# Sliding-window attention and gated MLP on one core: another order of the first attention steps, a fifth column group moved once per head, and a last row normed on VectorE

## The chip, the cores and the metric

The kernel runs on one core of a Trainium2 chip. The metric is the device time in microseconds of one execution. A core has five engines with instruction queues of their own: TensorE (PE in the profile, its weight loads PEld), VectorE (DVE), ScalarE (ACT), GpSimd (POOL) and SyncE (SP). SP, POOL and ACT also issue DMAs.

## The reference, cut to what matters

`x` has 2048 rows of 576 values in bf16. Four layers follow each other, A, B, A, B, each added to `x`:

```
def _A_ref(x, wqkv, wo):        # x is layer-normed first
    H = 32; Dh = 18; W, dil = (8, 2)
    q, k, v = split(x @ wqkv)
    idx = pos[:, None] - off[None, :]            # off = 0, 2, ..., 14
    logits = einsum('bhsd,bhswd->bhsw', q, kg) * scale, masked where idx < 0
    attn = softmax(logits);  o = einsum('bhsw,bhswd->bhsd', attn, vg)
    return o @ wo

def _B_ref(x, w_in, w_sp, b_sp, w_out):          # x is layer-normed first
    z = gelu(x @ w_in)                           # 576 -> 4608
    z1 = z[..., :Fh];  z2 = layernorm(z[..., Fh:])
    g = einsum('ts,bsf->btf', w_sp, z2) + b_sp
    return (z1 * g) @ w_out
```

## The kernel before, in words

**Layer A.** The normed input lies transposed in `xnT` (5 chunks of the 576 columns; row blocks of 128). The even and the odd rows of `x` are kept as two halves, so that the dilated window becomes a dense one. Queries and keys of all heads go into the tile `QK` (`[128, 2, 8, 2048]`: keys or queries, eight groups of four heads, rows); the rows of a head that hold no query or key hold a pattern (`win_pat`) which makes the window's mask part of the matrix product.

The way into `QK` has three stages. `PG(d, qk, cc)` computes one column group `d` of 128 columns (`d` = 0 to 4; the fifth has only 64 query and 64 key columns, which are computed together in one product of 128 rows), for keys or queries (`qk`), and one block `cc` of 512 rows, in a PSUM bank `pp`. `evac` copies the bank to a staging tile `stg` (for `d` of 3 and 4 in the first layer it is a piece of `win2a`, lent until that weight is loaded). When a stage is full, a DMA for each head moves its 18 columns to their place in `QK`. Column group 0 holds heads 0 to 7, group 1 heads 7 to 14, group 2 heads 14 to 21, group 3 heads 21 to 28, group 4 heads 28 to 31. For group 4 the keys and queries of a head lie on other partitions of the stage (64 apart), and two DMAs move a head.

The PSUM banks `pp` come from `PT_tile`, a ring: in this part of the layer it is Y, Y, PT, PT, PT, five banks, so that the fifth request after one gets the same bank again. A bank is free again when every instruction that reads it is done.

The attention runs over 17 row tiles and two halves of the heads: step `s` is tile `s // 2` and half `s % 2` (heads 0 to 15, then 16 to 31), 34 steps. `L_mm(s)` multiplies keys by queries into `L_ps`, `EXP(s)` takes the exponential on ACT, `PV(s)` multiplies by the values, and DVE divides by the sums. In the loop, step `s` issues `L_mm(s+1)`, `EXP(s+1)`, `PV(s)` and then what a table holds for the step: the remaining `PG` of rows 1024 to 2047, `VW` (values of a tile), `WO` (output product), loads and stores. `L_mm(0)` and `EXP(0)` stand between the `PG` units of the list `pre`, ahead of the loop.

Everything in the layer is in `manual_schedule`: each engine takes its instructions in the order in which the code issues them.

The first layer (`li == 0`) begins with layer norms: `S_` (statistics, `B_` and `G_`), `R_` (the reciprocal root, its power on POOL), `A_` (norm on DVE), then a transpose on PE (`T_pe`) or by DMA on SP's queue (`T_`). `rows[2]` and `rows[3]` build the mask pattern, `load_pat` loads it, and `fill_window_rows(QK, 0)` writes it into half of `QK` with copies on DVE (L198). What follows on each queue there is set by these lines:

```
            self.fill_window_rows(QK, 0)
            S_(13, 14, 15)
            order = [(d, cc) for cc in range(2) for d in range(5)]
            for k_, (d, cc) in enumerate(order):
                for qk in ((1, 0) if d < 4 else (0,)):
                    PG(d, qk, cc, False, ...)
```

`False` is the argument `dve`: ACT evicts. In the second layer A (`li == 2`) the first sixteen units run in two groups of eight by `PG_run`, whose third argument lists the units that DVE evicts (the others are ACT's); then come

```
            self.fill_window_rows(QK, 1)
            for cc in range(2):
                PG(4, 0, cc, False, q2)
```

and eight `VW` units. In the first layer `fill_window_rows(QK, 1)` stands in the list `pre`, behind its fourth unit.

**Layer B.** `p1` (z2 with its norm), `p2` (z1 and the gate product, most of the time) and `p3`, the out stage: 16 row blocks, for each the product with `w_out`, the residual sum on DVE (`p3_finish`), and, when another layer A follows, the layer norm of the new row: statistics on DVE (`ln_stats`; the power and `nmr`, the negated mean times the reciprocal root, on POOL), the norm on ACT (`ln_xn`), and the transpose into `xnT`. The transpose of the last row block is issued inside the next layer A, between its two groups.

Of the kernel before, what the change touches and what calls it, by code (L numbers as in the profile page):

```python
# [63 lines left out]
class K:  # L64
# [275 lines left out]
    def layer_A(self, li):  # L340
# [44 lines left out]
        def q0_(t):  # L385
            return cfg.tiles[t][0]
# [55 lines left out]
        def PG(d, qk, cc, dve, queues=(nc.sync, nc.gpsimd), pp=None):  # L442
# [14 lines left out]
            if pp is None:  # L457
                pp = self.PT_tile([P, 512], f32, "pp")[:, :]
                for c in range(5):
                    PG_mm(pp, d, qk, cc, c, c == 0, c == 4)  # L460
            evac(stg[:, qk, gi * 512:(gi + 1) * 512], pp, dve)
            stg_left[key] -= 1
            if stg_left[key] == 0:
                stg_tiles.pop(key)
                cs = slice(cc * 512, (cc + 1) * 512) if alone else slice(cb * CBW, (cb + 1) * CBW)
                ss = slice(gi * 512, (gi + 1) * 512) if alone else slice(0, CBW)
                moves = []
                for h in range(d * P // DH, H):
                    a, b = max(h * DH, d * P), min((h + 1) * DH, (d + 1) * P)
                    if a >= b:  # L470
                        break
                    g, rg = divmod(h, 4)
                    q0, s0, n = 32 * rg + a - h * DH, a - d * P, b - a
                    if d < 4:
                        moves.append((QK[q0:q0 + n, :, g, cs], stg[s0:s0 + n, :, :]))
                    else:
                        for a_ in range(2):
                            moves.append((QK[q0:q0 + n, a_, g, cs], stg[64 * a_ + s0:64 * a_ + s0 + n, 0, ss]))
                for dst, src in moves:
                    dma_rr[0] += 1  # L480
                    self.dma(dst, src, eng=queues[dma_rr[0] % len(queues)])

        NST = 2 * NT
        L_tiles = {}
        owed = []
# [15 lines left out]
        def EXP(s):  # L501
            nk, nq = tdim(s // 2)
            for jp, L_ps in enumerate(L_tiles.pop(s)):
                Lv = L_ps[:].rearrange("p a (b c) -> p a b c", c=P)
                nc.scalar.activation(out=P_bufs[2 * jp + s % 2][:nk, :, :, 0:nq], in_=Lv[:nk, :, :, 0:nq], func=ACT.Exp,  # L505
                                     scale=scale)
# [4 lines left out]
        def PV(s):  # L511
# [3 lines left out]
            for jp, js in enumerate(((0, 1, 2), (3,))):  # L515
                for ftl in range(4):
                    for jj, j in enumerate(js):
                        idx = 4 * ftl + j
                        nc.tensor.matmul(O_ps[:, idx * (DH + 1):(idx + 1) * (DH + 1)],  # L519
                                         lhsT=P_bufs[2 * jp + s % 2][:nk, jj, ftl, :],  # L520
                                         rhs=v_ext[:nk, t, 16 * hf + idx, :], start=True, stop=True)
# [112 lines left out]
        if li == 0:  # L634
# [74 lines left out]
            for i in range(3):  # L709
# [5 lines left out]
                for t, hh in (((0, 0),), ((0, 1),), ((1, 0), (1, 1)))[i]:  # L715
                    VW(t, hh, False)
            B_(4)
            A_(3)
            G_(4)
            T_pe(3)  # L720
            for t in (2, 3):
                for hh in range(2):
                    VW(t, hh, False)
            x3 = sb.tile([P, 4, D], bf16, name="x_in3", tag="x_in", bufs=2)
            x_load(x3[:], 12, 4, nc.sync)
            stgs.append(x3[:].rearrange("p a b -> p (a b)")[:, 0:2 * CBW].rearrange("p (a b) -> p a b", a=2))
            S_(5)
            R_(4, 2)
            rows[2](nc.sync)
            A_(4, 5)  # L730
# [24 lines left out]
        else:  # L755
# [3 lines left out]
            for d0 in (0, 2):  # L759
                PG_run([(d, qk, cc) for d in (d0, d0 + 1) for cc in range(2) for qk in (1, 0)], qs,  # L760
                       (0, 1, 5, 7) if d0 == 0 else (1, 3, 5, 7),
                       None if d0 == 0 else lambda: nc.vector.memset(wqk4[64:128, :], 0.0))
# [40 lines left out]
        for k_, (t, hh) in enumerate(vws):  # L803
            assert vsteps[k_] <= 2 * t - 2 + hh
            at(vsteps[k_], VW, t, hh, vsteps[k_] >= PG_END - 2 and k_ % 2 == 0)
# [4 lines left out]
        for t in range(NT - 2):  # L810
            s = wo_steps[q0_(t) // P][0] - 1
            r = (q0_(t) + tdim(t)[1] - 1) // P - RING
            if t < NT - 3 and not in_ring(t):
                at(min(2 * t + 6, s), O_CP, t)
                assert r < 0 or wo_steps[r][1] < min(2 * t + 6, s)
            else:
                assert r < 0 or wo_steps[r][1] < 2 * t + 1
        tail_rows = []
# [37 lines left out]
        for k_, (d, qk, cc) in enumerate(pre):  # L856
            if k_ == (2 if li == 0 else 0):
                self.ring = ["PT"]
                L_mm(0)
                EXP(0)  # L860
# [26 lines left out]
    def layer_B(self, li):  # L887
# [259 lines left out]
        def p3_finish(i, acc):  # L1147
# [108 lines left out]
```

## Time and profile before

| what | value |
|---|---|
| time, median of 3 runs | 1162.35 us (1161.28 to 1163.54) |
| the profiled execution's own time | 1164.2 us |
| its span, first to last instruction | 1162.4 us |
| mean granted TensorE clock | 0.997 |
| PE busy | 1146.0 us (99%), 8163 instructions |
| DVE, ACT, POOL busy | 559.4 us, 339.0 us, 271.0 us |
| first layer A | 0 to about 125 us |
| first layer B | to about 588 us, its out stage from 517 us |
| second layer A | to about 696 us |
| second layer B | to the end |

A row of the timeline has the start, the busy time, the engine, the line of the kernel, the operation, what it writes and reads, how many instructions are merged in the row, and, in brackets, how long the engine was idle ahead of it and what released it. A row of the windows has the busy time of each engine in a stretch with its number of instructions, then the granted clock, the share of the DMA engines and their rate. A row of the chain has the start, the length and the work.

### The profile page before, as it was taken

What the parts mean: (1) busy time and instruction counts of PE and PEld (TensorE: products, weight loads), DVE (VectorE), ACT (ScalarE), POOL (GpSimd) and SP (SyncE); (2) the same over time, 40 slices, a digit from 0 to 9 for tenths busy, and PEclk for the clock granted to TensorE, in tenths of its full rate; (3) what the DMA queues carried; (4) which work ended last, traced back from release to release, by engine and by line L of the source; (5) the groups of instructions that cost most, each with busy time, mean ns of one, the idle gap of its engine ahead of it and who ended that gap; (6) DMA issues with size and microseconds to landing.
All of it is one profiled execution on the core that took longest, in us unless ns stands there. A gap on an engine that the chain in (4) does not pass through costs nothing.

```text
span 1162.4 us, 19969 instructions
## 1 busy us (share of the span) xinstructions
PE 1146.0 (99%) x8163; PEld 610.5 (53%) x8258; DVE 559.4 (48%) x1183; ACT 339.0 (29%) x503; POOL 271.0 (23%) x375
## 2 busy tenths in 40 slices
PE   9899999999999999999999999999999999999998
PEld 5467544444444444457755774444444444444677
DVE  8679888322233222235475888862322223322321
ACT  5499455011110111102247884541011110011000
POOL 3769855000000000001163776540000000000000
PEclk9899999999999999999999999999999999999999
DMA  9599796000000000049656997920000000001332
GB/s 214 114 177 291 199 219 132 23 12 12 12 2 11 12 12 1 19 138 297 172 102 117 229 245 183 259 55 4 8 12 12 12 12 1 12 1 47 114 104 74
DMA packets 184600, 106.59 MB, mean 92 GB/s; under 512 B 136201, under 2 KB 165545, under 8 KB 184509
## 3 DMA queue, kind: packets, MB, share of 16 engines
q1 hardware_dynamic: 171821, 86.04, 32.4%
q0 software_dynamic: 6096, 13.38, 4.4%
q10 hardware_dynamic: 6592, 5.90, 1.7%
q8 instruction: 64, 1.05, 0.4%
q14 instruction: 27, 0.22, 0.1%
HBM read 42.54 MB, written 21.77 MB: 55 GB/s over the span
## 4 chain that ended last, share of the span: by engine, by line
PE 94%; issue 1%; POOL 1%; ACT 1%; DVE 1%; DMA 1%; SPq 0%; ACTq 0%; DVEq 0%; POOLq 0%
PE pg L1094 43%; PE po L1143 12%; PE pz L946 6%; PE pz L1070 6%; PE pz1s L1070 6%; PE pzs L946 6%; PE pp L422 5%; PE pw L587 3%; PE O_ps L519 3%; PE pv L411 3%; PE L_ps L496 2%; POOL QK L78 1%; ACT P_sb L505 1%; DMA x_in<-in_A_x_dram 0%; DVE QK L198 0%
## 5 line engine op out<-in xcount | busy, mean ns | idle before, releaser
L1094 PE MATMUL pg<-Wq,Z 128*128 128x512 bf16 x2260 | 497.9, 379 | 2.5
L1094 PEld LDWEIGHTS <-Z 128*128 128x128 bf16 x2304 | 225.4, 98 | 271.8
L1098 DVE TENSOR_TENSOR g_tmp<-pg,ln_xn 128x512 f32<-128x512 f32 x144 | 99.6, 692 | 420.8 <-PE pg L1094 418.8
L1089 ACT ACTIVATE z1T<-pz 128x1024 bf16<-128x1024 f32 x36 | 34.9, 1021 | 500.8 <-PE pz L1070 500.8
L78 POOL DMA_DIRECT2D wout<-in_B_w_out_dram x4 | 4.3, 1073 | 598.8 <-PE pg L1094 598.8
L1143 PE MATMUL po<-wout,Z 128*128 128x288 bf16 x1152 | 141.4, 286 | 0.0
L505 ACT ACTIVATE P_sb<-L_ps 128x1440 bf16<-128x1440 f32 (+3 forms) x136 | 125.1, 972 | 23.0 <-PE L_ps L496 21.4
L1143 PEld LDWEIGHTS <-Z 128*128 128x128 bf16 x1152 | 112.7, 98 | 28.8
L946 PEld LDWEIGHTS <-xnT 128*128 128x128 bf16 (+1 forms) x800 | 68.2, 97 | 75.3 <-issue 9.7
L1099 DVE TENSOR_TENSOR Z<-g_tmp,z1T 128x512 bf16<-128x512 f32 x144 | 99.7, 692 | 13.0 <-DVE g_tmp L1098 0.9
L995 DVE BATCH_NORM_STATS2 z_st<-zp 128x6 f32<-128x512 bf16 (+1 forms) x160 | 91.5, 618 | 14.6 <-ACT zp L993 14.3
L1070 PEld LDWEIGHTS <-w 128*128 128x128 bf16 (+1 forms) x640 | 53.7, 97 | 74.0 <-issue 13.6
L422 PE MATMUL pp<-xnT,wqk_sb 128*128 128x512 bf16 (+1 forms) x313 | 76.4, 385 | 1.1 <-issue 0.2
L1153 DVE TENSOR_TENSOR x_new<-po,xo 128x288 f32<-128x288 f32 (+1 forms) x64 | 28.8, 455 | 88.4 <-PE po L1143 82.6
L1070 PE MATMUL pz<-xnT,w 128*128 128x512 bf16 (+1 forms) x316 | 66.3, 380 | 0.2
L1070 PE MATMUL pz1s<-xnT,w 128*128 128x512 bf16 (+1 forms) x310 | 64.9, 379 | 0.9 <-issue 0.8
L258 POOL TENSOR_SCALAR ln_xn<-x_new,ln_mv,ln_rstd 128x576 bf16<-128x576 f32 x28 | 64.1, 2289 | 2.6
L946 PE MATMUL pzs<-win2a,xnT 128*128 128x512 bf16 (+1 forms) x235 | 58.6, 358 | 0.4 <-issue 0.3
L946 PE MATMUL pz<-win2a,xnT 128*128 128x512 bf16 (+1 forms) x233 | 58.3, 357 | 0.4
L993 ACT ACTIVATE zp<-pz 128x1024 bf16<-128x1024 f32 (+2 forms) x56 | 36.6, 720 | 64.5 <-PE pz L946 64.5
L1019 POOL TENSOR_SCALAR Z<-zp,z_mv,z_rstd 128x256 bf16<-128x256 bf16 x32 | 54.4, 1701 | 3.8 <-POOL z_rstd L1011 0.4
L78 POOL DMA_DIRECT2D QK<-stg x76 | 46.9, 621 | 35.2 <-DVE stg L403 17.2
(124 smaller groups left out, 951.6 us busy)
## 6 DMA issues: line engine op xcount, KB each, us to landing
xres<-x_new SPq DMA_DIRECT2D x44, 288.0 KB
xo<-xres SPq DMA_DIRECT2D x32, 288.0 KB
wout<-in_B_w_out_dram POOLq DMA_DIRECT2D x4, 1296.0 KB, 7.9
xn_rows<-ln_xn SPq DMA_DIRECT2D x28, 160.0 KB
w<-in_B_w_in_dram SPq DMA_DIRECT2D x16, 256.0 KB
QK<-stg POOLq DMA_DIRECT2D x51, 72.0 KB, 4.7
xo<-xres SPq DMA_DIRECT2D x6, 576.0 KB
QK<-stg SPq DMA_DIRECT2D x37, 72.0 KB
```

Of the source, the lines that this page charges most:

```text
L78: return eng.dma_start(out=out, in_=in_)
L258: e.tensor_scalar(out=xn[:nrows, 0:D], in0=x_t[:nrows, :], scalar1=mv[:nrows, 0:1], scalar2=rstd[:nrows, 0:1], op0=ALU.subtract, op1=ALU.mult)
L422: nc.tensor.matmul(pp, lhsT=w, rhs=self.xnT[r0:r1, c, cc * 512:(cc + 1) * 512], start=start, stop=stop, tile_position=(r0, 0))
L505: nc.scalar.activation(out=P_bufs[2 * jp + s % 2][:nk, :, :, 0:nq], in_=Lv[:nk, :, :, 0:nq], func=ACT.Exp, scale=scale)
L946: nc.tensor.matmul(out[:, o0:o0 + n], lhsT=self.xnT[r0:r1, c, r * P:(r + 1) * P], rhs=win2(c)[r0:r1, w0:w0 + n], start=start, stop=stop, t ...
L995: nc.vector.bn_stats(out=st[:, x // 512, :], in_=zp[:, x:x + min(512, w0 + n - x)])
L1019: eng.tensor_scalar(out=Z[:, b0:b1, i, :], in0=zv[:, b0:b1, :], scalar1=mv[:, 0:1], scalar2=rstd[:, 0:1], op0=ALU.subtract, op1=ALU.mult)
L1070: nc.tensor.matmul(outs[a_], lhsT=w1[r0:r1, c, sub * P:(sub + 1) * P], rhs=self.xnT[r0:r1, c, q * 512:(q + 1) * 512], start=start, stop=st ...
L1094: nc.tensor.matmul(pg[:, :], lhsT=Z[:, jj, i, sub * P:(sub + 1) * P], rhs=Wq[q][:, i, :], start=(i == 0), stop=(i == NS - 1))
L1098: nc.vector.tensor_tensor(out=tmp[:], in0=pg[:, :], in1=bsp[:, qs], op=ALU.add)
L1099: nc.vector.tensor_tensor(out=uT(jj)[:, sub, qs], in0=tmp[:], in1=z1Ts[jj, sub][:, qs], op=ALU.mult)
L1143: nc.tensor.matmul(acc[hh], lhsT=u_rows(j, i), rhs=wouts[j // NJH][:, j % NJH, hh * 288:(hh + 1) * 288], start=(j == 0), stop=(j == NJ - 1))
```

## The change

Five edits, in the layers A and at the end of the first layer B's out stage.

1. `evac` of column group 4 is split into two: partitions 0 to 63 of the bank go to `stg[0:64, 0]` on the engine that evicted before, partitions 64 to 127 to `stg[0:64, 1]` on the other one of ACT and DVE. Keys and queries of a head then lie on the same partitions, and one DMA moves a head. This holds in both layers A.
2. The first layer A takes its steps in the order `seq`: 0, 2, 4, 1, 3, 5 in place of 0 to 5, and 18 ahead of 17. `pos` is a step's place; buffers by parity and the copies out of `o_slot` go by it. `L_mm(0)` comes behind the third unit of `pre` and no longer behind the second.
3. In the first layer's beginning, `rows[2]` stands ahead of `A_(3)`, the statistics of block 4 behind the units `VW` of tiles 2 and 3, and `VW(2, 0)` ahead of the transpose of block 3.
4. In the second layer A, DVE evicts units 4 and 6 of the first `PG_run`, where it had 0, 1, 5 and 7.
5. The last row block of the first layer B is normed on DVE, without `nmr` on POOL.

```diff
@@ PG
-            evac(stg[:, qk, gi * 512:(gi + 1) * 512], pp, dve)
+            gs = slice(gi * 512, (gi + 1) * 512)
+            if d < 4:
+                evac(stg[:, qk, gs], pp, dve)
+            else:
+                for a_ in range(2):
+                    evac(stg[0:64, a_, gs], pp[64 * a_:64 * a_ + 64, :], dve if a_ == 0 else not dve)
...
-                    if d < 4:
-                        moves.append((QK[q0:q0 + n, :, g, cs], stg[s0:s0 + n, :, :]))
-                    else:
-                        for a_ in range(2):
-                            moves.append((QK[q0:q0 + n, a_, g, cs], stg[64 * a_ + s0:64 * a_ + s0 + n, 0, ss]))
+                    moves.append((QK[q0:q0 + n, :, g, cs], stg[s0:s0 + n, :, ss]))
...
         NST = 2 * NT
+        seq = list(range(NST))
+        if li == 0:
+            seq[0:6] = [0, 2, 4, 1, 3, 5]
+            seq[17:19] = [18, 17]
+        pos = {s: p_ for p_, s in enumerate(seq)}
@@ layer A, li == 0
-            B_(4)
+            rows[2](nc.sync)
             A_(3)
-            G_(4)
+            VW(2, 0, False)
             T_pe(3)
-            for t in (2, 3):
-                for hh in range(2):
-                    VW(t, hh, False)
+            VW(2, 1, False)
+            VW(3, 0, False)
+            VW(3, 1, False)
...
-            S_(5)
+            S_(4, 5)
             R_(4, 2)
-            rows[2](nc.sync)
             A_(4, 5)
@@ layer A, li == 2
                 PG_run([(d, qk, cc) for d in (d0, d0 + 1) for cc in range(2) for qk in (1, 0)], qs,
-                       (0, 1, 5, 7) if d0 == 0 else (1, 3, 5, 7),
+                       (4, 6) if d0 == 0 else (1, 3, 5, 7),
@@ the loop
-            if k_ == (2 if li == 0 else 0):
+            if k_ == (3 if li == 0 else 0):
                 self.ring = ["PT"]
                 L_mm(0)
                 EXP(0)
...
             if s + 1 < NST:
-                L_mm(s + 1)
-                EXP(s + 1)
-            PV(s)
+                L_mm(seq[s + 1])
+                EXP(seq[s + 1])
+            PV(seq[s])
@@ layer B, p3_finish
-                mv, rstd, nmr = self.ln_stats(p3, x_new, P)
-                xns[i] = self.ln_xn(x_new, P, mv, rstd, nmr, eng="act")
+                on_dve = i == NS - 1
+                mv, rstd, nmr = self.ln_stats(p3, x_new, P, want_nmr=not on_dve)
+                xns[i] = self.ln_xn(x_new, P, mv, rstd, nmr, eng="dve" if on_dve else "act")
```

More of the change, by code (lines that the diff above doesn't have):

```diff
@@ L504, in EXP @@
                 Lv = L_ps[:].rearrange("p a (b c) -> p a b c", c=P)
-                nc.scalar.activation(out=P_bufs[2 * jp + s % 2][:nk, :, :, 0:nq], in_=Lv[:nk, :, :, 0:nq], func=ACT.Exp,
+                nc.scalar.activation(out=P_bufs[2 * jp + pos[s] % 2][:nk, :, :, 0:nq], in_=Lv[:nk, :, :, 0:nq], func=ACT.Exp,
                                      scale=scale)
@@ L519, in PV @@
                         nc.tensor.matmul(O_ps[:, idx * (DH + 1):(idx + 1) * (DH + 1)],
-                                         lhsT=P_bufs[2 * jp + s % 2][:nk, jj, ftl, :],
+                                         lhsT=P_bufs[2 * jp + pos[s] % 2][:nk, jj, ftl, :],
                                          rhs=v_ext[:nk, t, 16 * hf + idx, :], start=True, stop=True)
@@ L803, in layer_A @@
         for k_, (t, hh) in enumerate(vws):
-            assert vsteps[k_] <= 2 * t - 2 + hh
+            assert vsteps[k_] < pos[2 * t + hh] - 1
             at(vsteps[k_], VW, t, hh, vsteps[k_] >= PG_END - 2 and k_ % 2 == 0)
@@ L810, in layer_A @@
         for t in range(NT - 2):
-            s = wo_steps[q0_(t) // P][0] - 1
+            s, done = wo_steps[q0_(t) // P][0] - 1, pos[2 * t + 1]
             r = (q0_(t) + tdim(t)[1] - 1) // P - RING
             if t < NT - 3 and not in_ring(t):
-                at(min(2 * t + 6, s), O_CP, t)
-                assert r < 0 or wo_steps[r][1] < min(2 * t + 6, s)
+                at(min(done + 5, s), O_CP, t)
+                assert done + 2 < s and (r < 0 or wo_steps[r][1] < min(done + 5, s))
             else:
-                assert r < 0 or wo_steps[r][1] < 2 * t + 1
+                assert r < 0 or wo_steps[r][1] < done
         tail_rows = []
```

## Prediction

> **What bounds the kernel now.** I read the page's head first, then the windows around the two attention layers, the chain of waits there, and last the timeline of each engine, for the order of its queue.
>
> ```profile
> span 1162.4 us, 19969 instructions
> PE 1146.0 (99%) x8163; PEld 610.5 (53%) x8258; DVE 559.4 (48%) x1183; ACT 339.0 (29%) x503; POOL 271.0 (23%) x375
> 46.60:51.40 4.80, 1.34 (x17) 0.56 (x16) 2.17 (x2) 0.76 (x2) 3.27 (x3) 0.85 0.43 97
> 51.40:56.80 5.40, 5.18 (x58) 2.36 (x58) 2.12 (x5) 3.41 (x4) 1.56 (x4) 0.50 0.04 8
> ```
>
> TensorE is busy for 99% of the span, so what the change can win or lose is PE's idle time, and slow clock behind it. The windows show the largest such place: from 46.6 to 51.4 us PE works 1.34 of 4.80 us, and then 5.40 us run at half clock (0.50). The chain and the timeline tell why.
>
> ```profile
> 44.83 4.03 issue
> 48.87 0.50 POOL QK L78
> 49.37 1.80 DMA QK<-win2a
> ...
> 46.63 0.35 PE L496 MATMUL L_ps<-QK 32*128 32x128 bf16 x12
> 50.22 0.28 PE L496 MATMUL L_ps<-QK 32*128 32x128 bf16 x1 [2.78 <-DMA QK<-win2a]
> 51.21 0.28 PE L496 MATMUL L_ps<-QK 32*128 32x128 bf16 x1 [0.21 <-DMA QK<-win2a]
> 51.42 0.60 PE L519 MATMUL O_ps<-v_ext,P_sb 128*128 128x19 bf16 x16
> 57.06 0.39 PE L496 MATMUL L_ps<-QK 32*128 32x120 bf16 x16
> ...
> 40.31 9.56 POOL L78 DMA_DIRECT2D QK<-win2a  x9
> 44.15 4.62 DVE L198 COPY QK<-win_pat 128x4096 bf16<-128x4096 bf16 x4
> ```
>
> Step 1 needs heads 28 to 31, whose moves are the last of POOL's nine issues; one of those stood still for the 4.03 us in which DVE copied the pattern. Step 1 began at 46.63 and its last products ran at 51.21. A step in the steady loop takes 1.91 us (the row of 24 ACT instructions below, two to a step, 22.89 / 12). Undisturbed, the third pair of `L_mm` would have begun at 46.63 + 2 x 1.91 = 50.45; it began at 57.06. This place costs **6.6 us**.
>
> **Part 1: steps 0, 2, 4 first, one move per head.** The heads of column group 4 are now needed at the fourth place, two steps (3.8 us) later; the group has four moves where it had eight, so POOL issues seven instead of nine. Seven were issued by 44.83 (the stop begins there). The old wait goes: **-6.6 us**, its half clock included. What is late next I looked for in the two halves that group 4's eviction is cut into. One goes to DVE, in DVE's order. Here is that order in the first layer, with the ACT evictions that mark PE's units (one in 1.08 us):
>
> ```profile
> 23.66 0.59 ACT L405 CAST win2a<-pp 128x512 bf16<-128x512 f32 x1 [0.49 <-PE pp L422]
> 27.97 0.59 ACT L405 CAST stg<-pp 128x512 bf16<-128x512 f32 x1 [0.49 <-PE pp L422]
> 29.05 0.59 ACT L405 CAST stg<-pp 128x512 bf16<-128x512 f32 x1 [0.49 <-PE pp L422]
> ...
> 26.33 2.36 DVE L198 COPY QK<-win_pat 128x4096 bf16<-128x4096 bf16 x2 [1.89 <-issue]
> 28.82 2.35 DVE L198 COPY QK<-win_pat 128x4096 bf16<-128x4096 bf16 x2
> 31.30 0.81 DVE L673 BATCH_NORM_STATS2 ln_st<-x_in 128x6 f32<-128x288 bf16 x2
> 34.00 0.21 DVE L676 BATCH_NORM_AGGREGATE lnx_mv<-ln_st 128x2 f32<-128x12 f32 x1
> 34.24 0.17 DVE L685 TENSOR_SCALAR lnx_rstd<-lnx_mv 128x4 f32<-128x4 f32 x1
> L403 DVE CAST stg<-pp 128x512 bf16<-128x512 f32 x6 | 3.9, 686 | 1.6 <-PE pp L422 1.6
> 29.65 9.64 POOL L78 DMA_DIRECT2D QK<-stg  x15 [5.43 <-ACT stg L405]
> 40.32 0.72 PE L496 MATMUL L_ps<-QK 32*128 32x128 bf16 x16
> ```
>
> The eviction at 23.66 is the ninth unit, group 4 of the first rows. In the code the pattern copies and the statistics of blocks 13 to 15 come ahead of all `PG` units, so the DVE half waits in the queue behind them until 34.2 and takes 0.69 more (686 ns, DVE's whole bank; a half has the same 512 elements in a partition, so I take the same; between 0 and this is what it could be). The bank is thus free at 34.95. The ring has five banks: the fifth request after this unit is the key unit of group 2, second rows. Its eviction stands at 29.05, and PE begins it 1.08 and the drain ahead, at about 27.8. In the changed kernel PE must stop there until 34.95: **+7.2 us**. Behind PE stand the rest of the projection, eight `VW` units, `pre`, and every step.
>
> The pattern's copies don't come earlier: `load_pat` is issued on SP behind the transposes of blocks 4 to 7, and these still need `A_(4)`; moving `rows[2]` ahead and block 4's statistics back is the same work in another order, so `A_(4)` moves by less than block 4's 1.0 us (0.81 + 0.21, rows of 31.30 and 34.00). I take 0 for it. In that opening PE gains at most the 0.39 us that it waits ahead of block 3's transpose (next fence), since `VW(2, 0)` fills it; the gain is eaten by the stop, whose end DVE sets: **0**. SP gets the two DMAs of `rows[2]` ahead of the load of blocks 12 to 15; both are early.
>
> ```profile
> 10.53 0.42 DVE L693 TENSOR_SCALAR ln_xn<-x_in,lnx_mv,lnx_rstd 128x576 bf16<-128x576 bf16 x1
> 11.00 0.45 PE L700 MATMUL pt<-ident,ln_xn 128*128 128x128 bf16 x5 [0.39 <-DVE ln_xn L693]
> 49.00:49.80 0.80, 0.00 (x0) 0.00 (x0) 0.00 (x0) 0.00 (x0) 0.80 (x2) 1.00 0.17 46
> 49.80:56.80 7.00, 5.93 (x60) 2.66 (x61) 2.12 (x5) 3.77 (x4) 1.63 (x5) 0.51 0.08 17
> 57.55 22.89 ACT L505 ACTIVATE P_sb<-L_ps 128x1440 bf16<-128x1440 f32 x24 [0.93 <-PE L_ps L496]
> ```
>
> A stop of 7.2 us brings half clock as the old one did: the clock fell some 2.8 us after PE's twelve products ended (46.98 to 49.8) and was back at about 56.7, 5.3 us after dense work had begun again (51.42). Half of 5.3: **+2.6 us**. The Trainium skill, "TensorE: Matmul & The Clock Gate", Part 1, has it that the gate looks at free-running windows of about 3.4 us, halves the clock after an idle one and restores it after a busy one; by that the half clock would last between 3.4 and 6.8 us and cost 1.7 to 3.4, an estimate from that page, and the rows above agree with it.
>
> While PE stands, nothing else becomes late for it: POOL has the moves of groups 0 and 1 (part of the 15 issues in 9.64 us) to make meanwhile, and group 2's then wait for PE instead of the other way round; the first `L_mm` comes at about 34.95 + 12.5 (from 27.8 to 40.32 now) + 2.6 + 1.1 (one more unit ahead) = 51.2, the second 5 us behind it, by which time the moves have had over 6 us.
>
> In the loop ACT evicts half of a bank twice more, at the places 0 and 11, where DVE had both evictions whole. The row of 24 exponentials has no gap in 22.89 us: ACT is as full as PE there. The price lies between 0 (hidden) and 2 x 0.59; the rows without a gap speak for the upper end: **+0.9 us**. Steps 17 and 18 are swapped at a place where the chain shows no wait for `QK`: 0.
>
> First layer: -6.6 + 7.2 + 2.6 + 0.9 = **+4.1 us**.
>
> **Part 2: the border of the first layer B and the second layer A.**
>
> ```profile
> 589.66 2.16 POOL L238 TENSOR_TENSOR ln_rstd<-ln_rstd,neg_half 128x1 f32<-128x1 f32 x1 [3.50 <-DVE ln_rstd L237]
> 591.91 2.40 POOL L242 TENSOR_SCALAR ln_nmr<-ln_mv,ln_rstd 128x1 f32<-128x1 f32 x1
> 594.34 0.87 ACT L252 ACTIVATE ln_xn<-x_new,ln_nmr,ln_rstd 128x576 bf16<-128x576 f32 x1 [7.00 <-POOL ln_nmr L242]
> 594.38 1.28 DVE L403 CAST stg<-L_ps 128x512 bf16<-128x512 f32 x2
> 596.39 2.53 PE L422 MATMUL L_ps<-xnT,wqk_sb 128*128 128x512 bf16 x11 [0.40 <-ACT stg L405]
> 585.25 0.55 POOL L238 TENSOR_TENSOR ln_rstd<-ln_rstd,neg_half 128x1 f32<-128x1 f32 x1 [3.50 <-DVE ln_rstd L237]
> ```
>
> Now POOL's two small operations are stretched to 2.16 and 2.40 us while DVE copies the pattern (the one of the row before took 0.55), and ACT stands behind them for 7.00 us. All PE loses is the 0.40 us at 596.39. With the norm on DVE, ACT is free to evict units 0 to 3 as PE ends them: **-0.4 us**. DVE waits for POOL (0.55 and signals), norms (0.9; bounds: the 0.42 at 10.53, from bf16, and a good 1.1 for ACT's 0.87 with the copy behind it), and so ends the copies 1.9 us later than at 594.38, at 596.3; its units 4 and 6 are out at 597.7. PE needs the first of those banks in the second group's fifth chunk, 16 x 0.215 us after 596.0, at 599.4. That margin of 1.7 us is the cover; without it the loss would be DVE's delay beyond it.
>
> Then the halves again:
>
> ```profile
> 605.18 4.66 DVE L198 COPY QK<-win_pat 128x4096 bf16<-128x4096 bf16 x4
> 606.53 5.06 PE L411 MATMUL pv<-wv_sb,xnT 128*128 128x288 bf16 x40
> 646.69 1.83 ACT L505 ACTIVATE P_sb<-L_ps 128x1440 bf16<-128x1440 f32 x2 [0.60 <-PE L_ps L496]
> ```
>
> `fill_window_rows(QK, 1)` precedes both group-4 units on DVE, until 609.84. The fifth request after the first of them is the fourth `VW` unit: 606.53 + 3 x 0.61 = 608.4. With everything 0.4 earlier, it wants to begin at 608.0 and gets the bank at 609.4 + 0.69 = 610.1: **+2.1 us**; too short for the clock. ACT's halves in this loop fall at its places 11 and 12, where ACT sits idle 0.60 us ahead of an exponential, as much as a half takes (0.59): 0. Second layer: **+1.7 us**.
>
> **The sum.** +4.1 + 1.7 = +5.8. The profiled execution took 1164.2 us for a span of 1162.4; so 1170.0 for a profiled one. The median of the runs is 1.85 lower, 1162.35, and gives **1168.2 us**. A time within 0.2% of before (2.3 us) is about what cannot be told from no change.
>
> **The rivals.** (a) *The halves don't hold PE*: the bank is not the one asked for, or DVE gets to it before its copies. Then the old stall is gone and nothing replaces it: -6.6 - 0.4 + 0.9 = -6.1, 1156.2 us. It decides if DVE's half of the ninth unit ends by 27.8. For it: ACT freed that bank in time until now, and the two loop orders are plainly aimed at the 6.6 us. Against it: DVE's rows from 26.33 to 34.24 follow one another as in the code, with only 0.2 us of idle between them. The Trainium skill, "TensorE: Matmul & The Clock Gate", the note on engine queue depths under the 32x32 array, says that VectorE's queue is strictly first in, first out; by that this rival falls, and DVE's rows agree. Chance 0.10. (b) *The stops are there, but the clock stays up* or comes back at once, and ACT's halves are hidden: 7.2 - 6.6 - 0.4 + 2.1 = +2.3, 1164.7 us. Against it: 49.80 to 56.80 at 0.51 after a shorter idle. Chance 0.08. (c) *The second layer's stop is missing* because its banks turn round otherwise: +3.7, 1166.1 us. Chance 0.07. (d) *The stop drags more along*: DVE's pattern copies 0.6 later, half clock for 6.8 us, POOL's moves of groups 2 to 4, issued only behind the delayed units, late for step 0 or 2: +0.6 + 0.8 + up to 2, about 1171.5 us. For it: POOL issued from 29.65 to 49.9 (40.31 + 9.56) with little between in the old order; against: PE is later by more than these moves. Chance 0.10.
>
> **How the numbers follow.** The forecast has 0.65 of the chance; its own terms move it by the clock (1.7 to 3.4), ACT (0 to 1.2) and the stop (0.5 either way), 1166 to 1170. The range takes in (b), (c) and most of (d): 1164.0 to 1171.5, and leaves out (a) and the tail of (d). Faster by over 0.2% is (a) and a little of unseen gain: 0.11; within 0.2% is the lower part of (b): 0.07; slower 0.82.
>
> **What would show it.** Right: no wait for `QK` by step 1, but an idle PE from 27.5 to 35, released by a DVE eviction of group 4 that stands behind the statistics of block 15; clock 0.5 for some 5 us from there; the second `L_mm` at about 56; in the second layer PE idle for 2 us among the first `VW` units, released by DVE behind L198, and no ACT wait for `ln_nmr` at the border. Wrong: PE dense from 14 to 45, or the wait of 50.22 still there.

## The result, and the profile after

The changed kernel takes 1170.4 us (median of 16 runs, 1168.77 to 1180.64), the kernel before in the same series 1161.52 us (16 runs, 1157.44 to 1169.98). The ratio is 1.0082, with a 95% interval of 1.0062 to 1.0102: slower by 8.9 us. Its profiled execution took 1168.77 us, its span is 4.6 us above that of before, 1162.4. Why the profiles differ by 4.6 and the medians by 8.9 is the main point of what follows.

The head of the page after:

```profile
span 1167.0 us, 20039 instructions
PE 1151.8 (99%) x8258; PEld 610.9 (52%) x8258; DVE 561.1 (48%) x1187; ACT 341.2 (29%) x507; POOL 258.5 (22%) x362
```

PE is still busy for 99%. Its busy time reads 5.8 us more than before, where 1146.0 stood, but that can't be taken for work: 8258 matmuls are recorded here and 8163 there. One and the same kernel of the experiments below (both halves on one engine) reads 1149.5 us with 8258 records in a span of 1158.0, and 1145.5 us with 8163 in a span of 1164.9. The timeline of the changed kernel shows the first stop (start, busy time, engine, line, what is done, idle time ahead and its releaser):

```profile
19.79 8.37 PE L422 MATMUL pp<-xnT,wqk_sb 128*128 128x512 bf16 x38
32.64 8.11 PE L422 MATMUL pp<-xnT,wqk_sb 128*128 128x512 bf16 x25 [4.48 <-DVE win2a L403]
...
23.88 0.58 ACT L405 CAST win2a<-pp 64x512 bf16<-64x512 f32 x1 [0.49 <-PE pp L422]
23.99 2.36 DVE L198 COPY QK<-win_pat 128x4096 bf16<-128x4096 bf16 x2
26.47 2.36 DVE L198 COPY QK<-win_pat 128x4096 bf16<-128x4096 bf16 x2
31.66 0.21 DVE L682 BATCH_NORM_AGGREGATE lnx_mv<-ln_st 128x2 f32<-128x12 f32 x1
31.90 0.69 DVE L403 CAST win2a<-pp 64x512 bf16<-64x512 f32 x1
...
48.82 0.40 PE L502 MATMUL L_ps<-QK 32*128 32x128 bf16 x16
```

PE ends at 28.16 (19.79 + 8.37) and stands until 32.64, and what releases it is DVE's half of group 4. That half ran at 31.90 directly behind the statistics of block 15, though ACT's half of the same bank was out at 24.46 (23.88 + 0.58). PE was not dense from 27.5 on, and there is no wait for `QK` any more in the first steps. The windows behind the stop (length, then busy time of PE, PEld, DVE, ACT, POOL, then the granted clock):

```profile
27.50:35.00 7.50, 3.02 (x10) 1.05 (x8) 5.00 (x14) 0.82 (x3) 5.98 (x9) 0.73 0.89 195
35.00:37.50 2.50, 2.50 (x7) 0.91 (x6) 0.00 (x0) 0.95 (x2) 0.00 (x0) 0.50 0.25 44
37.50:40.50 3.00, 3.00 (x14) 1.32 (x13) 0.00 (x0) 1.36 (x3) 2.21 (x4) 0.94 0.33 58
```

The clock is 0.50 throughout the second window and comes back 0.36 us into the third (3.00 x 0.06 x 2), at 37.86, which is 5.2 us after PE set out again. Half of that is lost: 2.6 us.

In the loop, ACT's halves are in the way:

```profile
56.25 0.67 DVE L403 CAST win2a<-pp 64x512 bf16<-64x512 f32 x1
56.95 0.58 ACT L405 CAST win2a<-pp 64x512 bf16<-64x512 f32 x1 [0.97 <-DVE win2a L403]
58.98 0.41 PE L502 MATMUL L_ps<-QK 32*128 32x128 bf16 x16 [1.34 <-ACT P_sb L511]
...
79.02 0.58 ACT L405 CAST win2a<-pp 64x512 bf16<-64x512 f32 x1 [0.41 <-DVE win2a L403]
81.05 0.39 PE L502 MATMUL L_ps<-QK 32*128 32x120 bf16 x16 [1.33 <-ACT P_sb L511]
```

ACT's half does not only take its own 0.58 us: it waits for DVE's half of the same bank, and the exponentials stand behind both. The step at 58.98 follows the one before it (55.63) by 3.35 us, the one at 81.05 by 2.85 (from 78.20), where 1.91 is the pace: 1.43 + 0.94 = 2.4 us.

The second layer, first two rows of before, then those of after:

```profile
587.85 2.75 PE L422 MATMUL L_ps<-xnT,wqk_sb 128*128 128x512 bf16 x11
611.53 0.40 PE L496 MATMUL L_ps<-QK 32*128 32x128 bf16 x16
```

```profile
590.93 2.75 PE L422 MATMUL L_ps<-xnT,wqk_sb 128*128 128x512 bf16 x12
593.32 0.58 DVE L258 TENSOR_SCALAR ln_xn<-x_new,ln_mv,ln_rstd 128x576 bf16<-128x576 f32 x1 [0.73 <-POOL ln_rstd L238]
595.12 1.56 ACT L405 CAST stg<-L_ps 128x512 bf16<-128x512 f32 x3 [4.70 <-PE pp L422]
598.91 2.75 PE L422 MATMUL L_ps<-xnT,wqk_sb 128*128 128x512 bf16 x12
...
607.71 4.65 DVE L198 COPY QK<-win_pat 128x4096 bf16<-128x4096 bf16 x4
612.39 1.30 DVE L403 CAST stg<-pp 64x512 bf16<-64x512 f32 x2
613.13 3.22 PE L411 MATMUL pv<-wv_sb,xnT 128*128 128x288 bf16 x25 [2.08 <-DVE stg L403]
616.29 0.40 PE L502 MATMUL L_ps<-QK 32*128 32x128 bf16 x16
```

The norm of the last row stands on DVE, ACT no longer waits for `ln_nmr`, and the second group begins at 598.91 without a wait. But PE then waits 2.08 us for DVE's halves behind the pattern's copies. From the layer's first product to its first `L_mm` it was 23.68 us and is 25.36.

With these terms the two profiles add up: -6.6 (the old wait) + 4.48 + 2.6 + 2.4 + 1.68 = 4.56, and the spans differ by 4.6. Taken by stages, the first layer ends 3.08 us later (127.94 against 124.86, where its terms give 2.88), the stretch just named takes 1.68 more, and what is behind it 0.16 less; the account is good to some 0.2 us.

### The profile page after: what moved, and what is told of

It is laid out like the page before. It is cut to its first block, busy times and chain, and to the rows that moved or that the text cites. A ratio compares the mean times of both kernels' runs of the same rounds, so it can differ in the third digit from the quotient of the medians.

```text
span 1167.0 us, 20039 instructions
## 1 busy us (share of the span) xinstructions
PE 1151.8 (99%) x8258; PEld 610.9 (52%) x8258; DVE 561.1 (48%) x1187; ACT 341.2 (29%) x507; POOL 258.5 (22%) x362
## 4 chain that ended last, share of the span: by engine, by line
PE 94%; DVE 3%; ACT 1%; DMA 1%; issue 1%; POOL 0%; SPq 0%; DVEq 0%; ACTq 0%
PE pg L1099 43%; PE po L1148 12%; PE pz L951 6%; PE pz L1075 6%; PE pz1s L1075 6%; PE pzs L951 6%; PE pp L422 4%; PE pw L593 3%; PE pv L411 3%; PE O_ps L525 3%; PE L_ps L502 2%; DVE QK L198 1%; ACT P_sb L511 1%; DVE ln_st L679 1%; PE L_ps L422 1%
## 5 line engine op out<-in xcount | busy, mean ns | idle before, releaser
L511 ACT ACTIVATE P_sb<-L_ps 128x480 bf16<-128x480 f32 (+3 forms) x136 | 125.1, 972 | 15.8 <-PE L_ps L502 14.4
```

The costliest lines, as they stand in the source:

```text
L511: nc.scalar.activation(out=P_bufs[2 * jp + pos[s] % 2][:nk, :, :, 0:nq], in_=Lv[:nk, :, :, 0:nq], func=ACT.Exp, scale=scale)
```

## The experiments

**Where the profiles differ at all.** Layer B takes the same in every profile: from its first `pz` product to the next layer's first product it is 462.99 or 463.00 us in all of them, and what is behind the first `L_mm` of the second layer takes 550.7 to 551.6. So each execution can be read by two numbers, the end of the first layer and the stretch of the second layer named above. This table is worked out from the rows of the first `pz` product, of the second layer's first product and of its first `L_mm`:

| kernel | pattern copies begin | first layer ends | second layer, to `L_mm(0)` |
|---|---|---|---|
| before | 26.33 | 124.86 | 23.68 |
| before, a second profile | 24.12 | 121.40 | 23.67 |
| changed | 23.99 | 127.94 | 25.36 |
| both halves on one engine | 24.62 | 121.02 | 23.12 |
| the same, a second profile | 24.32 | 127.96 | 23.12 |
| first layer's early halves on ACT | 24.35 | 124.95 | 25.36 |
| second layer's halves on ACT | 28.07 | 131.07 | 23.12 |
| loop's halves on DVE | 24.21 | 130.75 | 27.04 |
| order of steps alone | 23.98 | 118.77 | 23.68 |
| border alone | 23.93 | 120.59 | 23.12 |
| one engine, later copies | 24.32 | 120.81 | 23.12 |
| two moves | 24.20 | 121.69 | 23.12 |
| order and border | 23.89 | 122.00 | 23.12 |
| one engine, old opening | 23.73 | 130.15 | 23.12 |

The last column is a property of the kernel, to 0.01 us. The border's two edits are worth 23.68 - 23.12 = 0.56 us, the second stop costs 25.36 - 23.12 = 2.24. The middle column is not a property of the kernel: the same first layer ends at 124.86 and 121.40, another at 121.02 and 127.96.

**Which half holds PE.** In the edit of group 4, one expression says which engine takes the second half. Four variants:

```
-  evac(stg[0:64, a_, gs], pp[...], dve if a_ == 0 else not dve)
+  ... dve)                                                  # one engine
+  ... dve if a_ == 0 or (li == 0 and not dve) else not dve) # first layer's early halves on ACT
+  ... dve if a_ == 0 or (li > 0 and not dve) else not dve)  # second layer's halves on ACT
+  ... dve if a_ == 0 else True)                             # loop's halves on DVE
```

> As the changed kernel, but in the first layer, ahead of the loop, both halves of a group-4 bank are ACT's; the second layer and the loops stay as changed. Theory: takes away the first stop (4.48 us in the profile of the changed kernel) and the half clock behind it (2.6 us): 7.1 us less than 1170.4, so 1163.3 us; PE dense from 14 to 46 us, the first L_mm at about 41.4. Rival (the half clock comes from elsewhere): 4.5 less, 1165.9. Rival (DMAs or order cost): no change, 1170.

Measured: 1166.1 us (11 runs), ratio 1.0035 [1.0015, 1.0056], against 1.0082 for the changed kernel: 0.47% or 5.5 us less. Its timeline:

```profile
13.97 19.59 PE L422 MATMUL pp<-xnT,wqk_sb 128*128 128x512 bf16 x90
41.63 0.40 PE L502 MATMUL L_ps<-QK 32*128 32x128 bf16 x16
...
50.47 1.24 PE L422 MATMUL pp<-xnT,wqk_sb 128*128 128x512 bf16 x5 [1.14 <-DVE win2a L403]
52.53 0.40 PE L502 MATMUL L_ps<-QK 32*128 32x128 bf16 x16 [0.82 <-ACT P_sb L511]
...
72.32 0.35 DVE L553 COPY oT<-o_slot 128x600 bf16<-128x600 bf16 x1 [1.68 <-DMA o_slot<-o_t]
73.38 0.79 PE L411 MATMUL pv<-wv_sb,xnT 128*128 128x288 bf16 x5 [0.73 <-DVE o_t L533]
75.97 0.59 PE L502 MATMUL L_ps<-QK 32*128 32x120 bf16 x16 [1.81 <-ACT P_sb L511]
```

PE has no stop from 13.97 on, the granted clock is 1.00 from 30 to 50 us, and the first `L_mm` comes at 41.63 in place of 48.82: 7.19 us earlier, which is the stop and its half clock (4.48 + 2.6). That cause is shown, by the timeline; the total lies between the 7.1 us of the theory and the 4.5 of its first rival. By the end of the layer 2.99 of it are left (124.95 against 127.94). PE waits in the loop for 1.14 + 0.82 + 0.73 + 1.81 = 4.50 us, where the changed kernel has 1.34 + 1.33 = 2.67. The halves, still on two engines there, are one part of it: ACT's stands behind DVE's. Late DMAs are another, since they made DVE's half itself late: it waited 0.53 us for a move into `QK` ahead of the first of these places, and 1.68 us for a DMA transpose (row of 72.32) ahead of the other. And behind the last two waits the clock falls, where the changed kernel has 1.00 in the same window:

```profile
60.00:80.00 20.00, 17.46 (x335) 10.15 (x334) 12.10 (x29) 16.15 (x20) 10.68 (x19) 0.91 1.11 149
```

0.09 of 20.00 us is 1.8, so that 3.6 of the missing 4.2 us are accounted for.

> As the changed kernel, but in the second layer, ahead of the loop, both halves of a group-4 bank are ACT's; the first layer and the loops stay as changed. Theory: takes away the stop of 2.1 us among the VW units there: 1168.3 us against 1170.4 of the changed kernel. Rival (that stop is hidden by slack later in the layer): no change, 1170.

Measured: 1169.83 us (6 runs), ratio 1.0082 [1.0055, 1.0109], the same as the changed kernel. The interval is 3.1 us to each side, so the total cannot show the 2.2 us. The profile can:

```profile
28.07 2.36 DVE L198 COPY QK<-win_pat 128x4096 bf16<-128x4096 bf16 x2 [3.65 <-DMA win_pat<-win_period]
36.73 7.14 PE L422 MATMUL pp<-xnT,wqk_sb 128*128 128x512 bf16 x25 [8.27 <-DVE win2a L403]
...
612.19 5.06 PE L411 MATMUL pv<-wv_sb,xnT 128*128 128x288 bf16 x40
```

All 40 `VW` products run in one row, without a stop. And it happened to catch a late pattern: DVE waited 3.65 us for the load `win_pat`, the copies began 4.08 us later than in the profile above, the half followed them, and the first stop grew from 4.48 to 8.27. The stop ends later by as much, 36.73 - 32.64 = 4.09: its end is set by the load's landing.

> As the changed kernel, but in the loops both halves of a group-4 bank are DVE's; ahead of the loops as changed. Theory: ACT waits for DVE's half and delays the next exponential at the places 0 and 11 of the first layer, 1.43 and about 1.0 us by the profile of the changed kernel; that goes, 2.4 us less, 1168.0 us; in the second layer nothing. Rival (DVE's second half of 0.69 us is as late for PE there as ACT's was): no change, 1170.

Measured: 1174.94 us (6 runs), ratio 1.012 [1.0097, 1.0143], slower than the changed kernel: a miss. The two waits for ACT are gone. The fourth `L_mm` follows the third by 1.94 us (57.03 behind 55.09) in place of 3.35, which shows that ACT's half was the first of the two delays. At the second place the step still takes 2.72 us (78.26 to 80.98) against 2.85, with small waits for DVE and for a DMA in it, so there it isn't shown. And another wait has come:

```profile
86.28 0.35 DVE L553 COPY oT<-o_slot 128x600 bf16<-128x600 bf16 x1 [3.30 <-DMA o_slot<-o_t]
87.04 0.77 PE L411 MATMUL pv<-wv_sb,xnT 128*128 128x288 bf16 x5 [3.12 <-DVE x_new L596]
...
611.86 2.00 PE L411 MATMUL pv<-wv_sb,xnT 128*128 128x288 bf16 x15
615.95 4.89 PE L411 MATMUL pv<-wv_sb,xnT 128*128 128x288 bf16 x25 [2.09 <-DVE stg L403]
```

DVE stands in its queue at the copy out of `o_slot`, for a DMA transpose that has not landed, and PE stands behind DVE's next eviction. How much of the extra time the median owes to this isn't shown by one profile. The last row is told of at the end.

> The changed kernel with one thing taken back: both halves of a group-4 bank are evicted by one engine (ACT ahead of the loops, DVE in them), everything else of the change stays. Theory (the half on the other engine waits in that engine's queue and holds the bank): both stops of PE, the half clock and ACT's gaps in the loop go, and the old wait at step 1 stays away. From the profile of before: -6.6 (step 1) -0.4 (border) = -7.0, plus at most 0.3 for ACT's second half ahead of the loop (2 x 0.58 against PE's 1.08 a unit): 1154.5 to 1155 us against 1161.5. If the old wait costs less in most executions than in the profiled one, up to 1158. Rival one (the larger single move per head, or the new order of steps, is what costs): still slower than before, 1165 or more. Rival two (the opening or the border costs): likewise above 1162.

Measured: 1166.54 us (12 runs, 1158.89 to 1173.2), ratio 1.004 [1.0016, 1.0065]. Both stops and the long waits for ACT (over 1 us) are gone in its profile (span 1158.0, mean granted clock 1.00), 9.0 us less than the changed one; but that was one of its fastest executions, and the median keeps only 0.42% or 4.9 us of it. The theory's 1154.5 to 1158 us is missed even by the fastest run, and the median lies where the rivals had it. Another execution:

> The kernel with both halves on one engine once more, for another profiled execution: the first was one of the fastest (1159.8 us) of a median of 1166.5. Theory (DVE waits in the loop for an o_slot transpose, and PE for DVE, with half clock behind it): PE waits of over 2 us in the first layer's loop, between the places 12 and 20, released by DVE instructions that stand behind the copy out of o_slot. Rival (the slow executions lose their time elsewhere, in the second layer or in B): the loop of the first layer looks as in the first profile.

It took 1166.7 us, and shows where the time is given back. First SP's and DVE's queue, PE, then a window:

```profile
62.36 1.35 SPq L544 DMA_TRANSPOSE o_slot<-o_t  x1
69.99 2.02 SPq L544 DMA_TRANSPOSE o_slot<-o_t  x1
...
70.59 0.35 DVE L553 COPY oT<-o_slot 128x600 bf16<-128x600 bf16 x1 [1.04 <-DMA o_slot<-o_t]
83.22 0.34 DVE L553 COPY oT<-o_slot 128x600 bf16<-128x600 bf16 x1 [5.32 <-DMA o_slot<-o_t]
83.98 1.36 PE L411 MATMUL pv<-wv_sb,xnT 128*128 128x288 bf16 x5 [4.27 <-DVE x_new L596]
```

```profile
80.00:90.00 10.00, 6.02 (x89) 4.00 (x89) 5.17 (x17) 4.11 (x6) 7.12 (x8) 0.66 1.13 136
```

PE loses 4.27 us at 83.98, and the granted clock of 0.66 in that window says that half clock follows. The layer ends 6.9 us later than in the first profile of the same kernel (127.96 against 121.02), which is the whole difference of the two spans, 1164.9 and 1158.0.

**Is the old wait there at all?** A second profile of the kernel before:

> The kernel before once more, for another profiled execution. The first one had an old wait of 4.5 us with half clock behind it, and a mean clock of 0.997; most executions of before show a clock of 0.998 to 1.000. If the half clock is what tells them apart, this one has a wait at step 1 of under 4 us and little or no half clock, and a span near 1160. If not, the wait is as long as before.

```profile
24.12 2.36 DVE L198 COPY QK<-win_pat 128x4096 bf16<-128x4096 bf16 x2 [0.27 <-issue]
...
27.44 9.68 POOL L78 DMA_DIRECT2D QK<-stg  x15 [3.81 <-ACT stg L405]
38.13 4.65 POOL L78 DMA_DIRECT2D QK<-win2a  x8
42.98 0.51 POOL L78 DMA_DIRECT2D QK<-win2a  x1 [0.19 <-issue]
...
47.08 0.23 PE L496 MATMUL L_ps<-QK 32*128 32x128 bf16 x1 [0.41 <-DMA QK<-win2a]
50.74 0.39 PE L496 MATMUL L_ps<-QK 32*128 32x120 bf16 x16
...
78.40 0.77 PE L411 MATMUL pv<-wv_sb,xnT 128*128 128x288 bf16 x5 [1.04 <-DVE x_new L590]
```

It took 1161.47 us, as good as the median. The pattern came 2.2 us earlier than in the first profile, POOL was done with its moves of group 4 at 43.49 and not at 49.87, and step 1 waits 0.41 us. The `L_mm` at 50.74 is the one that stood at 57.06: the 6.6 us are missing here but for 0.3, and so is the slow clock (mean granted clock 1.00). Not all of this reaches the end of the layer, which comes 3.46 us earlier (121.40 against 124.86). The other 2.86 are lost on the way, most of them around 80 us: PE waits 1.04 at 78.40 for DVE, which had waited 1.54 for a DMA transpose, and 0.86 at 80.92 for a move into `QK`, and the steps there are slower.

Which of the two profiles is the ordinary one can be read from the granted clocks. The first has 0.997, by its 7.00 us at 0.51. Of 80 further executions of this kernel, those that ran beside the experiments, 17 have 0.997 or less: half clock of that length is in about a fifth of them at most. Of the 16 executions of the changed kernel all have 0.993 to 0.997.

> The kernel before with the new order of steps alone (0, 2, 4, 1, 3, 5, then 18 ahead of 17, and the first L_mm one unit later); group 4 is evicted whole by one engine and has two moves per head, the opening and the border are as before. Theory one (PE is what bounds the loop, the old wait at step 1 is lost time): that wait shrinks to under 1 us, since the moves land at 51.2 in the profile of before and place 3 wants them at 50.4; the time falls by most of the old wait, to 1156 to 1158 us. Theory two (formed on the run with both halves on one engine, 1166.5 us median from 1158.9 to 1173.2: what PE gains at step 1 is given back some steps later, where DVE waits for transposes of o_slot that the DMA queues bring late): no gain, 1161 to 1167, and a wider spread than before.

The edit is the list `seq`, its place numbers, and `L_mm(0)` one unit later, in the kernel before. Measured: 1161.67 us (12 runs, before 1163.77), ratio 0.9988 [0.9964, 1.0011]: no difference that can be told. In its profile the fourth `L_mm` is at 50.83:

```profile
50.83 0.40 PE L501 MATMUL L_ps<-QK 32*128 32x128 bf16 x16
```

It is not sooner than the 50.74 of the second profile of before: the order has nothing to take away there. What it does in an execution with a late pattern this run doesn't show. The wider spread of the second theory wasn't seen either (1158.15 to 1167.42 us, before 1158.53 to 1169.52).

> The kernel before with the border alone changed: the last row block normed on DVE, DVE evicts units 4 and 6 of the first group. By the prediction: PE's wait of 0.40 us there goes and nothing else moves: 1161.4 us against 1161.8, not to be told from no change. Rival (DVE, later by 1.9 us with its pattern copies, holds up PE in the second group): 1162.5 to 1164.

The edits 4 and 5 alone: 1161.56 us (12 runs, before 1163.77), ratio 0.9989 [0.9966, 1.0013]. Its first layer is that of before, and in its profile too PE has no wait for `QK` of 0.3 us or more at step 1, with pattern copies at 23.93.

**Whether the late transpose is the cause.** One edit on top of the variant with one engine:

```
-                at(min(done + 5, s), O_CP, t)
+                at(min(done + 7, s), O_CP, t)
```

> The changed kernel with both halves of group 4 on one engine, and the copies out of o_slot two places later in the loop (five places behind a tile's second step become seven). Theory: what the missing stops should have won is given back because VectorE stands in its queue at the copy out of o_slot until a late DMA transpose has landed (5.32 us ahead of the copy in one profile), with TensorE 4.27 us behind it and slow clock after that; two places are 3.8 us, so most of it goes and the median falls to 1158 to 1161 us, where the same kernel without this had 1166.54. Rival: the transposes are not what makes it slow (their lateness is a sign of other DMA traffic that delays moves or loads as well); then the median stays at 1164 to 1168 us.

Measured: 1165.11 us (12 runs, 1159.59 to 1171.38), ratio 1.0023 [1.0004, 1.0042]. That is in the rival's interval, not in the theory's. Its profile, an execution of 1159.59 us, has none of the waits at the copies between 70 and 88 us, and one of 1.30 us at 114.95. But seven of the twelve runs took over 1164 us, so these waits are at most a part of it, as far as a change of the median can tell; no slow execution of this variant was profiled.

**Which edit makes the first layer uneven.** Without the split between two engines, a table of two by two, all with the new order and border, each with its ratio to the kernel before. The edits are those of the diff, put back one at a time: with two moves group 4 is evicted whole, `evac(stg[:, qk, ...], pp, dve)`; the old opening has `B_(4)`, `G_(4)`, `rows[2]` and `VW(2, 0)` where they stood.

| | two moves per head | one move per head |
|---|---|---|
| opening of before | 1.0002 [0.9987, 1.0016] (order and border) | 1.0016 [0.9997, 1.0035] (old opening) |
| new opening | 1.0009 [0.9991, 1.0027] (two moves) | 1.0040 [1.0016, 1.0065] (one engine, above) |

> The changed kernel with group 4 evicted whole by one engine and moved twice per head, as before; the order of steps, the opening and the border are those of the changed kernel. Theory: neither stop of TensorE comes (no eviction of group 4 lies behind the pattern's copies), and the order gives the two moves time; if the single move or its use of the queues is what made the kernel with both halves on one engine slow, this one comes to 1160 to 1162 us. Rival: the opening (mask rows and the values of tile 2 ahead) is what makes it slow; then 1165 to 1168 us, as with the single move.

> The kernel before with the order of steps and the border's two edits (evictions of the first group, last row block normed on VectorE), without the single move and without the new opening. Each alone stood at 0.999 of before. Theory: the gains are independent and small, 0.4 us at the border and up to 2 in the order; together 1 to 2.5 us faster than before, a ratio of 0.998 to 0.999. Rival: they are nothing but noise, a ratio of 1.000 to 1.001.

> The changed kernel with both halves of group 4 on one engine and the opening of before: single move, order and border, nothing else. With the two runs above it makes a table of two by two: single move or not, new opening or not. If the single move is what costs, 1165 to 1168 us; if the opening costs, 1160 to 1162 us; if only both together cost, 1160 to 1162 us here and with two moves as well.

Medians in this order: 1163.51, 1161.23 and 1163.47 us (12 runs each), before 1161.65. Neighbours in the table can't be told apart; only the two ends of the diagonal are apart, and their intervals still touch at 1.0016. Order and border came out as the rival had it, as nothing but noise; the other two medians fell between the intervals set out for them and settle nothing. The profile of the variant with one move and the old opening is of one of its longer executions, 1168.9 us:

```profile
79.53 0.47 PE L502 MATMUL L_ps<-QK 32*128 32x120 bf16 x15 [1.53 <-DMA QK<-x_in]
85.40 0.35 DVE L553 COPY oT<-o_slot 128x600 bf16<-128x600 bf16 x1 [7.35 <-DMA o_slot<-o_t]
86.16 1.36 PE L411 MATMUL pv<-wv_sb,xnT 128*128 128x288 bf16 x5 [5.65 <-DVE x_new L596]
```

Here a move into `QK` is late as well as the transpose. What makes these DMAs late in some executions and not in others isn't settled. DVE's longest wait at a copy out of `o_slot` is 2.06 us in the six profiles with two moves per head; with one move it is 3.30, 5.32 and 7.35 in three of eight, and 1.68 or less in the others. That speaks for the single move, but so few profiles don't show it. And no version was shown to beat before: order and border together, the best candidate, came to 1.0002, where the second layer's 0.56 us are 0.05%.

## Why the prediction was right or wrong

Predicted were 1168.2 us in 1164.0 to 1171.5, slower with 0.82; measured 1170.4. The mechanisms were found where they were looked for. Two of the sizes were those of an untypical execution, a third was too small, and the errors partly cancel.

| step | predicted | profile after | what the runs add |
|---|---|---|---|
| old wait goes | -6.6 | -6.6 | -0.3 in a typical execution |
| first stop | +7.2 | +4.48 | 5.21 and 8.27 in two others |
| half clock | +2.6 | +2.6 | |
| ACT's halves | +0.9 | +2.4 | |
| border | -0.4 | } +1.68 | -0.56 |
| second stop | +2.1 | } | +2.24 |
| sum | +5.8 | +4.6 | medians: +8.9 |

**The old wait, -6.6: the mechanism held, the size failed.** The wait went, as said. But the step took the place of one profile as the place of every execution. By the two profiles of that kernel it hangs on when the pattern's copies begin: with copies at 26.33 POOL's last moves came too late for step 1, with copies at 24.12 they did not. That the landing of the pattern's load sets this beginning is named by the trace only for the copies at 28.07; for those at 26.33 it names no releaser. The `L_mm` that stood at 57.06 is at 50.74 in the second profile, and the prediction's own undisturbed figure was 50.45: 0.3 us is what the change can win there in an ordinary execution. Twelve of the thirteen other profiles have their copies between 23.73 and 24.62, and only one has a later pattern.

**The first stop, +7.2: place and cause right, size off for the same reason.** PE stopped at 28.16 (27.8 was said) until DVE's half behind block 15's statistics. The end of the stop was carried over from the same late profile; 2.3 us earlier copies end it 2.3 us earlier (32.64 in place of 34.95), and the second `L_mm` comes at 53.72, where about 56 was said. The two errors, 6.3 and 2.7 us, hang on one event and partly offset each other in the sum, -6.6 + 7.2 = 0.6 with a late pattern against -0.3 + 4.48 = 4.2 with an early one; the early one is the ordinary case, and that is 3.6 us of what the forecast lacked.

**Half clock, +2.6: right.** 5.2 us of it were seen after PE set out again, 5.3 said.

**ACT's halves, +0.9: mis-sized.** The step counted ACT's own time, at most 2 x 0.59. What it missed is that the halves of one bank don't run side by side: ACT's waits for DVE's, which has its own queue ahead of it, and the exponential waits for both: 2.4 us. For the first of the two places, 1.43 us, the variant with the loop's halves on DVE shows it; for the second it is read from the changed kernel's rows alone.

**Border, -0.4, and second stop, +2.1: right**, 0.56 and 2.24. The idle stretch is where it was put, among the first `VW` units, and released by DVE behind L198. "Too short for the clock" held in this profile, but not in every one (see the last section).

**The rivals.** (a), no hold of PE, fell with the rows of 31.90 and 32.64, (b) with the clock of 0.50, (c) with the row of 613.13. Of (d) the late pattern came in one profile; moves late for step 0 or 2 weren't seen in the changed kernel.

**The sum against the medians.** With ordinary executions on both sides, -0.3 + 4.48 + 2.6 + 2.4 + 1.68 = +10.9, 2 us more than measured. The profiles of the two first layers say the same from another side: ends at 127.94 and 131.07 with the change (the second layer's variant has the same first layer) against 124.86, 121.40 and 120.59 without, so 129.5 - 122.3 = 7.2 on average, and with the second layer's 1.68 it is 8.9. From five profiles this is a rough account. The 2 us between 10.9 and 8.9 fit the time that the kernel before loses later in the layer in its second profile (2.86 us, by waits for late DMAs); that its median execution loses them too isn't shown.

**Luck.** The forecast of the time came within 2.2 us, that of the difference within 3.1 (the median before fell by 0.83 from 3 runs to 16), by errors that cancel in part. It lacked 3.6 us from the late pattern and 1.5 from ACT's halves, and about 2 us that it didn't foresee went the other way.

**What stays open.** With the stops and the waits for ACT taken out, the kernel should have come out a little faster than before; it is 0.4% slower. In its second, longer profile the loss is a wait for late DMAs in the first layer's loop and half clock after it. Neither the place of the copies, nor the single move, nor the opening was shown to be the cause by itself.

## What to carry to other kernels

When a profile shows a wait for a DMA's landing, take a second profile before you price its removal: the row tells what that execution lost, and a cost that hangs on the same landing moves with it. If one eviction is cut between two engines, the bank comes free when the slower queue gets there, so look at what stands ahead of the half in each of the two queues, and at who waits behind it; here, one engine for both halves took away stops of 4.5 and 2.1 us. Look for a stretch that is the same in every profile of a kernel: an edit worth 0.56 us could be read there to a hundredth, though the total hides it.

## What the runs showed of the hardware

**Half a bank costs a whole eviction's time**: 64 x 512 took 0.69 us on DVE and 0.58 on ACT, the same as 128 x 512 (686 ns and 0.59): splitting by partitions makes the work of the two engines twice as much, not half.

**The halves ran one after the other** in the loop: DVE 56.25 to 56.92, ACT from 56.95. The trace names DVE's half as the releaser, so this is a wait between the two instructions. The Trainium skill, "PSUM — Partial Sum Buffer", section "PSUM bank collisions raise a hardware error", says that two engines collide in a bank only within the same 32 partitions, so that partitions 0 to 63 and 64 to 127 could be read at the same time; whether the kernel would gain by it wasn't tried.

**The same stop can cost half clock or not.** The second stop took 2.08 us in the changed kernel, and the 25 products behind it 3.22 us at full clock; in the variant with the loop's halves on DVE it took 2.09 us, and the same 25 products 4.89, with a granted clock of 0.62 in the first 3.35 us. That is 1.67 us for a pause that elsewhere was too short for the clock, and in the table it is the 27.04 beside 25.36. The Trainium skill, "TensorE: Matmul & The Clock Gate", Part 1, has the clock halved after an idle window of about 3.4 us: this pause was shorter than that, and the clock fell all the same in one of the three profiles that have it; here the measurement decides.

**A DMA transpose can take over 13 us to land**: issued at 69.99, its copy was released at 83.22 (the one before it 62.36 to 70.59), in a stretch for which the windows give a DMA share of 1.13.
